# Retention attention and SoLU layer on one core: another written-out order of all steps

## The chip, the core and the metric

The kernel runs on one core of one Trainium2 chip. Its engines work at once, each through its own instructions in their order: TensorE (PE) multiplies matrices, VectorE (DVE) and ScalarE (ACT) work on what PE leaves in PSUM, GpSimd (POOL) works on SBUF alone, and SyncE (SP) starts nearly all DMA transfers. The metric is the device time of one execution in microseconds; lower is better. Three runs of the kernel before took 214.81, 215.29 and 213.99 us (median 214.81).

## What is computed

Inputs are q, k and v (8 batches, 8 heads, 576 positions, 64 values per head), two matrices of 512x1024 and 1024x512, and a scale vector. Attention without softmax, with a decay by distance, makes 4608 rows of 512; a layer of two products with a gated softmax and a normalisation between them makes the output, in float32.

```python
scores = scale * np.matmul(q, k.transpose(0, 1, 3, 2))
Dmat = np.where(rel >= 0, gamma[:, None, None] ** rel[None, :, :], 0.0)
attn = np.matmul(scores * Dmat[None, :, :, :], v)
x = attn.transpose(0, 2, 1, 3).reshape(B * S, H * D)
h = x @ w_in
sm = softmax(h)            # over the 1024 columns
solu = h * sm
ln = (solu - mean(solu)) / np.sqrt(var(solu) + 1e-06) * g_ln
out = ln @ w_out
```

## The kernel before

The 576 positions of a batch are cut into two pieces of 256 and a tail of 64. With 8 batches this gives 18 items: 0 to 3 are the first pieces of four batches, 4 to 7 their second pieces, 8 their four tails together; 9 to 17 are the same for the other four batches. Each item has two halves of 128 rows. The products are in float16 with sums in float32.

An item goes through named steps (the functions marked `@step`); a step's numbers are the item, the half, and sometimes a part:

- Loads on SP: `lq`, `lk`, `lv` fetch q, k and v of an item in float32 (512 KB each); `wi` and `wo` fetch quarters of the two matrices. All go through one ring of 16 buffers of 512 KB.
- Casts to float16: `q`, `k`, `v` on DVE, ACT or POOL, each half by itself (line 197 with a decay table, lines 150 and 152 plain); `cwA`, `cwB` cast the first matrix, `ws` and `cw` scale and centre the second (`mean`, `mc` make its column mean).
- Attention: `tp` transposes q and k on PE (32 small products, line 239) and `qkT` copies the result out of PSUM; for eight items `dt`, a transposing DMA on SP, does both. `kp` multiplies k by v into the running state (32 products, line 290), `t` and `s32` add and decay that state (lines 305 and 314), `s16` casts it. `sc` makes scores (16 products, line 265), `mk` applies the triangular mask on DVE (four per item, line 276), `xv` and `xs` multiply masked scores by v (32 products, line 364) and the state by q (4, or 8 for a tail, line 349). `xT` copies the result out as float16.
- Layer: `mm1` multiplies by the first matrix (8 products of 512 columns, line 426) into two PSUM banks; `max` takes the row maximum on DVE (line 434), `exp` the exponential and its sum on ACT (line 449), `solu` the gated product and its sum on DVE (line 497), `nmu` and `sq` mean and squares, `w1`, `w2`, `pow` the factor of each row. `lpj` (32 products, line 584) with the copies `uTj`, or two transposing DMAs `du`, transpose the result; items 0 to 2 are centred first by `uc`. `mm2` multiplies by the second matrix (8 products, line 607), `osb` scales by the factor (lines 619 and 623), `st` stores.
- `warm:k` puts k products of zeros (line 726) into the next PSUM bank, into which the next step writes anyway. Nothing reads them.

Nothing is scheduled by a compiler. One text, `ORDER`, lists some 1000 steps; a loop at the end of the kernel calls them in that order, and each engine gets its instructions in that order. A letter behind a step chooses the engine (`@v` DVE, `@s` ACT, `@g` POOL). So the text fixes, for each engine and for SP's queue alike, what stands behind what; semaphores then hold an instruction until its inputs are there and its buffer is free. A second text, `BANKS`, gives one digit for each PSUM bank that a step takes, in the order of the steps. PSUM has eight banks; `tp`, `sc`, `kp`, `lpj` and `mm1` take two each, the others one.

```python
for word in ORDER.split():
    word, _, eng = word.partition("@")
    name, _, n = word.partition(":")
    idx = [int(x) for x in n.split(".")] if n else []
    STEP[name](*(idx + [None] * 3)[:3], eng)
```

Of the kernel before, what the change touches and what calls it, by code (L numbers as in the profile page):

```python
# [46 lines left out]
def kernel(  # L47
# [684 lines left out]
    def gx_(n, i, j, eng):  # L732
# [23 lines left out]
        wo:3 k:3.0@s wo:2 max:1.1 wo:1 w2:0 uc:0.0@v xv:2 max:1.0 lk:5 xT:2.0@s xs:2.1 exp:1.1
        xT:2.1@v warm:2 mm1:2.0 lv:4 q:3.1@g ws:0@g lk:4 exp:1.0 ws:1@g pow:0 q:3.0@g solu:1.1
        max:2.0 ws:2@g lpj:0 solu:1.0 ws:7@s ws:4@s ws:6@s ws:3@s exp:2.0 warm:4 mm1:2.1 uTj:0.0@v
        uTj:0.1@v w1:1@g kp:3 t:3.0@s nmu:1.1 max:2.1 tp:3 ws:5@s qkT:3.1@s s32:3.0 qkT:3.0@s
        q:4.0@g k:5.0@g mean s16:3.0@g t:3.1 nmu:1.0 solu:2.0 uc:1.1@s sc:3.0 mc@s sc:3.1 k:4.0@g  # L760
        uc:1.0@v k:4.1@s exp:2.1 mm2:0.0 v:4.1@v mk:3.1.0 mk:3.0.0 mk:3.0.1 cw:6@v lv:5 sq:1.1
        cw:0@v tp:4 lq:5 mm2:0.1 xs:3.1 mk:3.1.1 v:4.0@g osb:0.0@s osb:0.1@v xv:3 qkT:4.1@s
        qkT:4.0@s lk:7 solu:2.1 lv:6 warm:4 kp:4 cw:5@g v:5.1@g w1:2@g v:5.0@g xT:3.0@v t:4.0
        sc:4.0 mk:4.0.1 warm:2 sc:4.1 q:5.1@g mk:4.1.0 lpj:1 nmu:2.0 mk:4.0.0 sq:1.0 lq:6 lk:6
        xT:3.1@s st:0.1 mk:4.1.1 s16:1.1@s mm1:3.0 s32:4.0 uTj:1.0@s nmu:2.1 w2:1 uc:2.0@v cw:1@v
        max:3.0 s32:3.1 q:5.0@g v:6.0@g uTj:1.1@s warm:2 mm1:3.1 k:5.1@s cw:7@v sq:2.0 k:6.1@g
        q:6.1@s exp:3.0 v:6.1@g k:7.1@s t:4.1 pow:1 kp:5 mm2:1.1 k:6.0@g q:6.0@g max:3.1 osb:1.1@s
        s16:4.0@g s32:4.1 t:5.0 mm2:1.0 solu:3.0 tp:6 exp:3.1 solu:3.1 xs:4.1 xs:4.0 s32:5.0 lq:9
        st:0.0 osb:1.0@s xv:4 qkT:6.0@s xT:4.0@s xT:4.1@s uc:2.1@v kp:6 lpj:2 dt:5 qkT:6.1@v t:6.0
        uTj:2.0@s sc:5.1 mm1:4.0 nmu:3.1 t:5.1 mk:5.1.1 cw:2@g cw:4@g cw:3@v uTj:2.1@s sq:3.1  # L770
        sq:2.1 w1:3@v mk:5.1.0 sc:5.0 mm1:4.1 lk:9 s32:6.0 mk:5.0.0 max:4.0 exp:4.0 w2:2 lq:7
        q:9.0@g mm2:2.1 pow:2 s16:2.1@g mm2:2.0 mk:5.0.1 lv:8 s16:5.0@g st:1.1 max:4.1 osb:2.1@s
        exp:4.1 solu:4.0 nmu:3.0 sc:6.1 t:6.1 osb:2.0@s xv:5 q:7.0@g lv:7 lk:8 xs:5.0 xs:5.1 sc:6.0
        k:7.0@s s16:6.0@g xT:5.0@s solu:4.1 mk:6.1.1 q:7.1@g k:9.0@s s32:5.1 k:9.1@g lpj:3 mm1:5.0
        mk:6.1.0 mk:6.0.1 lpj:4 xT:5.1@s sq:3.0 mk:6.0.0 lq:8 xv:6 xs:6.0 k:8.1@g w2:3 dt:7
        uTj:3.1@s uTj:3.0@v v:7.0@v max:5.0 uTj:4.0@s xs:6.1 st:1.0 exp:5.0 mm2:3.1 q:9.1@g mm2:3.0
        xT:6.1 v:7.1@g uTj:4.1@v s32:6.1 pow:3 s16:4.1@s nmu:4.0 kp:7 nmu:4.1 solu:5.0 s16:3.1@s
        osb:3.1@s sq:4.0 warm:2 sc:7.1 xT:6.0 v:8.1@g q:8.1@g k:8.0@g sq:4.1 osb:3.0@s t:7.0
        mk:7.1.1 sc:7.0 s32:7.0 q:8.0@g w1:4@g mk:7.0.0 mm1:5.1 tp:8 mk:7.0.1 t:7.1 qkT:8.0@s
        max:5.1 mm1:6.0 exp:5.1 mk:7.1.0 qkT:8.1@s nmu:5.0 mm2:4.1 st:2.1 lk:10 lv:9 lq:10 w2:4  # L780
        max:6.0 st:2.0 pow:4 mm2:4.0 exp:6.0 s16:7.0@g q:10.0@s solu:5.1 v:9.1@g s32:7.1 solu:6.0
        sc:8.0 osb:4.1@s xv:7 q:10.1@g mk:8.0.0 v:8.0@g mk:8.0.1 sc:8.1 osb:4.0@s lpj:5 sq:5.0
        xs:7.1 uTj:5.1@s mk:8.1.0 xs:7.0 xT:7.0@v nmu:5.1 xT:7.1@v v:9.0@g sq:5.1 uTj:5.0@s mm1:6.1
        mm1:7.0 w1:5@g k:10.1@g max:6.1 s16:5.1@g s16:7.1@g mm2:5.1 mm2:5.0 exp:6.1 nmu:6.0
        mk:8.1.1 max:7.0 lv:10 lq:12 w2:5 st:3.0 dt:9 solu:6.1 st:3.1 nmu:6.1 exp:7.0 w1:6@g lpj:6
# [128 lines left out]
```

## Time and profile before

The profile is of one execution of 215.09 us; its span, from the first to the last instruction of the program, is 213.4 us.

| What | Before |
|---|---|
| Median of three runs | 214.81 us (213.99 to 215.29) |
| Profiled execution / its span | 215.09 us / 213.4 us |
| PE busy | 198.1 us (93%) |
| DVE busy | 186.6 us (87%) |
| ACT busy | 171.9 us (81%) |
| POOL busy | 141.6 us (66%) |
| Share of 16 DMA engines used by SP's queue | 91.2% |
| Products of zeros (line 726) | 62, 17.8 us busy |
| Mean granted PE clock | 0.99 |

"Busy" joins the times of an engine's instructions. PE's instructions overlap, so eight products of 512 columns that show 381 ns each follow one another every 216 ns or so. In the list of groups, a row names the line, the engine and the operation, what is written and read with the shapes, how often, the busy time, the mean of one, and then how long the engine had been idle just before and what ended that idle time. In the chain of waits a row is start, length and what ran then; "issue" is time in which the engine waited for nothing that the profile shows. In the timeline a row is start, length, engine, line and operation, and in brackets the idle time before it.

### The profile page before, as it was taken

The page shows a single profiled execution, that of the slowest core. Times are in us where ns is not written, and L with a number is a line of the kernel's source. Part 1 is how long each engine was busy: PE and PEld are TensorE (multiplying, and loading weights), DVE is VectorE, ACT ScalarE, POOL GpSimd, SP SyncE. Part 2 cuts the span into 40 slices and gives each one's busy share as a digit, 9 for nine tenths or more (in the row PEclk, how much of TensorE's full clock was granted, in tenths as well). Part 3 has the DMA queues.
Part 4 walks back from the last instruction along what each step waited for, and adds up shares of the span by engine and source line. Part 5 has one row for each costly group of instructions (what it writes and reads, how often), then busy time and mean ns, then how long its engine had stood idle before and what let it go on. Part 6 is the DMA issues. An engine that isn't in the chain of part 4 may idle for free.

```text
span 213.4 us, 7652 instructions
## 1 busy us (share of the span) xinstructions
PE 198.1 (93%) x3166; PEld 104.4 (49%) x3166; DVE 186.6 (87%) x334; ACT 171.9 (81%) x290; POOL 141.6 (66%) x222
## 2 busy tenths in 40 slices
PE   4999879899989989999969999999999999999990
PEld 1444454445446454564635455554555455454560
DVE  3586879999999998899979899999999999698960
ACT  3245789899979897898986988999999973779981
POOL 6496989589999999495789893748564861001130
PEclk9999969999999999999999999999999999999999
DMA  6999999999699799998999999799975977562654
GB/s 163 290 386 309 276 301 389 293 278 283 208 230 216 161 163 275 293 222 234 315 308 298 163 314 318 142 260 252 226 212 131 238 98 199 98 151 50 196 197 100
DMA packets 90530, 49.29 MB, mean 231 GB/s; under 512 B 29440, under 2 KB 84992, under 8 KB 90496
## 3 DMA queue, kind: packets, MB, share of 16 engines
q1 hardware_dynamic: 90128, 48.70, 91.2%
q8 instruction: 24, 0.39, 0.9%
q10 hardware_dynamic: 368, 0.11, 0.3%
q14 instruction: 10, 0.08, 0.2%
HBM read 32.55 MB, written 9.44 MB: 197 GB/s over the span
## 4 chain that ended last, share of the span: by engine, by line
PE 73%; DVE 9%; DMA 6%; SPq 4%; issue 3%; POOL 3%; ACT 1%; DVEq 0%
PE psum L607 28%; PE psum L426 24%; DMA ld<-in_q_dram 6%; PE psum L265 5%; PE psum L364 4%; PE psum L349 3%; SPq L173 3%; PE psum L584 3%; DVE nm L434 2%; DVE u L497 2%; PE psum L290 2%; SPq L647 1%; PE psum L239 1%; PE psum L726 1%; DVE uc L553 1%
## 5 line engine op out<-in xcount | busy, mean ns | idle before, releaser
L426 PE MATMUL psum<-w_in,xT 128*128 128x512 f16 x280 | 66.4, 381 | 0.4 <-DVE w_in L152 0.3
L607 PE MATMUL psum<-w_out,uTj 128*128 128x512 f16 (+1 forms) x248 | 55.6, 372 | 0.0
L449 ACT ACTIVATE e<-psum,nm 128x1024 f32<-128x1024 f32 x35 | 38.9, 1113 | 11.3 <-DVE nm L434 10.3
L434 DVE TENSOR_REDUCE nm<-psum 128x1 f32<-128x1024 f32 x35 | 42.6, 1216 | 2.1 <-PE psum L426 1.9
L607 PEld LDWEIGHTS <-uTj 128*128 128x128 f16 x296 | 27.9, 98 | 30.6 <-issue 1.0
L497 DVE SCALAR_TENSOR_TENSOR u<-psum,e 128x1024 f16<-128x1024 f32 x35 | 42.3, 1215 | 0.6
L517 ACT ACTIVATE sq<-u,nmu 128x1024 f16<-128x1024 f16 x35 | 40.3, 1151 | 0.7 <-DVE nmu L507 0.5
L426 PEld LDWEIGHTS <-xT 128*128 128x128 f16 x280 | 25.6, 98 | 29.7 <-issue 1.4
L540 POOL TENSOR_TENSOR rs<-w,mhalf 128x2 f32<-128x2 f32 x17 | 11.8, 694 | 35.0 <-DVE w L528 34.8
L197 POOL TENSOR_TENSOR qk<-ld,small 128x512 f16<-128x512 f32 x27 | 28.5, 1059 | 3.8 <-DMA ld<-in_q_dram 3.5
L197 POOL TENSOR_TENSOR v<-ld,small 128x512 f16<-128x512 f32 x28 | 30.4, 1090 | 0.3
L726 PE MATMUL psum<-s16s 128*128 128x512 f16 x62 | 17.8, 424 | 3.6 <-DVE s16s L854 3.1
L314 POOL TENSOR_TENSOR s32a<-t,small 128x256 f32<-128x256 f32 x16 | 9.8, 611 | 12.6 <-DVE t L305 7.1
L265 PE MATMUL psum<-qkT 64*64 64x128 f16 x576 | 15.0, 225 | 2.1 <-issue 1.7
L150 ACT COPY uTj<-psum 128x1024 f16<-128x1024 f16 (+1 forms) x17 | 16.3, 982 | 0.7 <-PE psum L584 0.4
L152 POOL CAST qk<-ld 128x512 f16<-128x512 f32 x24 | 15.1, 642 | 0.4 <-DMA ld<-in_k_dram 0.3
L265 PEld LDWEIGHTS <-qkT 64*64 64x64 f16 x576 | 9.9, 109 | 9.6 <-issue 7.8
L150 ACT CAST xT<-psum 128x512 f16<-128x512 f32 x23 | 12.9, 591 | 1.6 <-PE psum L364 1.5
L150 ACT CAST qk<-ld 128x512 f16<-128x512 f32 x20 | 12.1, 614 | 2.5 <-DMA ld<-in_k_dram 2.5
L150 ACT COPY qkT<-psum 128x1024 f16<-128x1024 f16 x12 | 11.9, 1018 | 1.0 <-PE psum L239 1.0
L314 POOL TENSOR_TENSOR s32b<-t,small 128x256 f32<-128x256 f32 x16 | 9.8, 612 | 2.9 <-DVE t L305 1.9
L607 PE MATMUL psum<-w_raw,uTj 128*128 128x512 f16 x48 | 11.2, 380 | 0.5 <-DVE t L305 0.5
(262 smaller groups left out, 334.6 us busy)
## 6 DMA issues: line engine op xcount, KB each, us to landing
ld<-in_v_dram SPq DMA_DIRECT2D x16, 512.0 KB, 7.2
ld<-in_q_dram SPq DMA_DIRECT2D x16, 512.0 KB, 7.3
ld<-in_k_dram SPq DMA_DIRECT2D x16, 512.0 KB, 7.1
ld<-in_moe_w_in_dram SPq DMA_DIRECT2D x4, 512.0 KB, 7.7
ld<-in_moe_w_out_dram SPq DMA_DIRECT2D x4, 512.0 KB, 6.9
ld<-in_v_dram SPq DMA_DIRECT2D x8, 128.0 KB, 4.7
ld<-in_k_dram SPq DMA_DIRECT2D x8, 128.0 KB, 5.3
ld<-in_q_dram SPq DMA_DIRECT2D x8, 128.0 KB, 5.4
```

The lines of the kernel that those rows point to most:

```text
L150: nc.scalar.copy(out=out, in_=in_)
L152: vec(eng).tensor_copy(out=out, in_=in_)
L197: vec(eng).tensor_tensor(out=to, in0=src, in1=tab[:, 8 * e : 8 * e + 8].unsqueeze(2).to_broadcast([P, H, D]), op=ALU.mult,)
L265: nc.tensor.matmul(out=s[o][cc, hp], lhsT=qkT_view(n, 1, c)[dd, e, hp], rhs=qkT_view(n, 0, c)[dd, :, hp], start=True, stop=True,)
L314: nc.gpsimd.tensor_tensor(out=s, in0=T["t", n, i], in1=gs.unsqueeze(2).to_broadcast([P, 4, D]), op=ALU.mult)
L426: nc.tensor.matmul(out=h[:, a], lhsT=s[:, d], rhs=w_in16[:, d, a * 512 : (a + 1) * 512], start=r == 1, stop=r == 4,)
L434: nc.vector.tensor_reduce(out=nm, in_=T[key("h", n, i, j)], axis=AX.X if j is not None else AX.XY, op=ALU.max, negate=True)
L449: nc.scalar.activation(out=flat(e, j), in_=T[key("h", n, i, j)], func=ACT.Exp, bias=T["nm", n, i], accum_out=s)
L497: nc.vector.scalar_tensor_tensor(out=flat(u, j), in0=T[key("h", n, i, j)], scalar=1.0, in1=flat(T[key("e", n, i, j)], j), op0=ALU.mult, op ...
L517: nc.scalar.activation(out=t, in_=T[key("u", n, i, j)], func=ACT.Square, bias=T["nmu", n, i], accum_out=ss)
L607: nc.tensor.matmul(out=o, lhsT=T["uT", n, i][:, c], rhs=wt[:, c, a : a + w], start=c == 0, stop=c == NF - 1,)
L726: nc.tensor.matmul(out=junk, lhsT=zeros[:, 0:P], rhs=zeros, start=True, stop=True)
```

## The change

Only the two texts change. `ORDER` has the same steps but for the products of zeros: these were 62 in 13 places and are 50 in 8 places; 19 stood ahead of the first `tp`, now 21 do, and behind it 43 become 29. All other steps stand in another order. 68 steps change engine: among them `s16` (7 from POOL to ACT, 8 back), `k` (5 POOL to ACT, 6 ACT to POOL, 2 to DVE), `q` (3 POOL to DVE), `xT` (4 DVE to ACT, 3 back), `t` (2 DVE to ACT). The loads have another order too: the first is `lk:0` where it was `lv:0`. `BANKS` has other digits, of the same number. The beginning, some stretches further on, and the digits:

```diff
     ORDER = """
-        lv:0 lq:0 v:0.0@v q:0.0@g gx lk:0 lq:1 k:0.0@s q:0.1@v v:0.1@v k:0.1@g warm:19 tp:0 q:1.1@g
-        warm:4 kp:0 qkT:0.0@v qkT:0.1@v lk:1 wi:2 warm:2 sc:0.0 t:0.0@v q:1.0@g mk:0.0.0 wi:3
-        warm:3 sc:0.1 mk:0.0.1 k:1.0@g wi:1 mk:0.1.0 mk:0.1.1 k:1.1@g wi:0 s32:0.0 t:0.1 s16:0.0@g
-        warm:2 tp:1 cwB:2@s cwB:3@g s32:0.1 lv:1 xv:0 qkT:1.1@s qkT:1.0@v xT:0.0@s xs:0.1 cwA:3@s
-        sc:1.0 warm:8 sc:1.1 xT:0.1@s cwB:1@v cwA:2@s lq:2 cwA:1@v cwB:0@g cwA:0@v mk:1.1.1
-        mm1:0.0.2 g32 v:1.1@g mm1:0.1 mk:1.1.0 v:1.0@v mk:1.0.0 max:0.1 lk:2 mk:1.0.1 mm1:0.0.0
-        kp:1 q:2.0@g t:1.0@s mm1:0.0.1 mm1:0.0.3 s32:1.0 max:0.0 q:2.1@g k:2.0@g lv:2 s16:0.1@s
-        exp:0.1 t:1.1 v:2.1@v s16:1.0@g v:2.0@g k:2.1@s solu:0.1 warm:8 tp:2 lk:3 kp:2 t:2.0@v xv:1
-        xs:1.1 exp:0.0 lv:3 qkT:2.0@s lq:3 lq:4 qkT:2.1@s xT:1.0@s solu:0.0 nmu:0.1 s32:1.1 s32:2.0
-        xT:1.1@s sc:2.1 wo:0 v:3.0@g v:3.1@g sc:2.0 mm1:1.1 mk:2.1.1 t:2.1 nmu:0.0 mk:2.0.0
...
+        lk:0 gx lq:0 k:0.0@s k:0.1@g q:0.0@v lv:0 lq:1 q:0.1@v warm:21 tp:0 v:0.1@v v:0.0@v kp:0
+        q:1.1@v t:0.0@v s32:0.0 qkT:0.1@v qkT:0.0@s lk:1 k:1.0@v q:1.0@g warm:6 sc:0.0 t:0.1 wi:2
+        k:1.1@s sc:0.1 wi:0 wi:3 s32:0.1 mk:0.1.0 warm:4 tp:1 mk:0.0.0 mk:0.0.1 cwB:2@s s16:0.0@s
+        mk:0.1.1 xv:0 cwA:2@g wi:1 qkT:1.1@v cwA:0@v cwB:0@g xT:0.0@v cwB:3@g qkT:1.0@s sc:1.0
+        mk:1.0.1 xs:0.1 cwA:3@s mm1:0.0.3 lv:1 cwA:1@g xT:0.1@v s16:0.1@g cwB:1@s v:1.1@g mk:1.0.0
+        sc:1.1 mm1:0.0.0 lq:2 lk:2 q:2.1@g q:2.0@g mk:1.1.0 mm1:0.1 v:1.0@v mk:1.1.1 k:2.0@g
+        max:0.1 exp:0.1 mm1:0.0.2 mm1:0.0.1 max:0.0 k:2.1@v kp:1 t:1.0@s warm:7 tp:2 s32:1.0 lv:2
+        solu:0.1 v:2.1@v exp:0.0 s16:1.0@g qkT:2.1@s qkT:2.0@s t:1.1 v:2.0@g nmu:0.1 solu:0.0
+        xs:1.1 lq:4 xv:1 lv:3 lq:3 lk:3 xT:1.0@s nmu:0.0 warm:2 sc:2.1 sc:2.0 mk:2.1.0 xT:1.1@s
+        kp:2 q:4.1@g q:4.0@g s32:1.1 mk:2.0.0 t:2.0@s mk:2.1.1 mk:2.0.1 uc:0.1@s sq:0.1 mm1:1.1
...
+        sc:4.1 q:6.0@s q:6.1@s mk:4.0.1 v:5.1@g mm2:1.0 exp:3.0 max:3.1 st:0.1 lv:6 mk:4.1.0
+        mk:4.1.1 mm2:1.1 xv:4 w1:2@g xs:4.1 v:6.0@g solu:3.0 k:6.0@s v:6.1@g osb:1.0@s exp:3.1
+        solu:3.1 dt:5 kp:5 t:5.0 osb:1.1@s xs:4.0 tp:6 st:1.0 s16:2.1@g cw:1@v st:0.0 sq:2.0 kp:6
+        xT:4.1@s t:6.0 warm:2 lpj:2 s32:5.0 qkT:6.1@v t:5.1 xT:4.0@s qkT:6.0@s uTj:2.1@s cw:4@g
+        sc:5.1 sc:5.0 uTj:2.0@s nmu:3.1 lq:8 mk:5.1.1 cw:7@v mk:5.1.0 sq:3.1 k:7.0@s sq:2.1 cw:3@v
+        mk:5.0.0 mm1:4.0 max:4.0 lv:8 cw:2@g w2:2 pow:2 s32:6.0 mm1:4.1 s16:5.0@g exp:4.0 s16:6.0@g
...
     BANKS = "".join(
         """
-        765473652176543201675354327654730167542354017654764532765426573102634127605704352713045760
-        173765432105672431732654301542376541073624501765432714053675342015427651034765201765437653
-        201765423475410326501457637210345763201763275463107567342017436520175642346571045762310745
-        760162376546501764532765476
+        765432765174630175237654736452316754230154673245345210765421076540156732473214065327640126
+        743025143761275463764521067531235076432016523767510643254016574237654103256743201765365721
+        034756201675436721045673210547623765401675473256107347652017654320176542365410756320174356
+        742340165746523765437653276
         """.split()
     )
```

More of the change, by code (lines that the diff above doesn't have):

```diff
@@ L756 @@
[L756 to L785, printed above, removed]
@@ L816 @@
-        w2:11 solu:12.1 t:15.1 xv:14 nmu:12.1 kp:16 solu:13.0 xs:14.0 sq:12.1 t:16.0 w2:12 mm1:13.1
-        pow:11 osb:11.1@s s32:15.1 s16:12.1@g s32:16.0 s16:11.1@g sc:15.1 xT:14.0 xT:14.1 nmu:13.0
-        sc:15.0 du:12.1 s16:16.0@g s16:15.0@s osb:11.0@s t:16.1 max:13.1 mk:15.0.1 pow:12 mk:15.0.0
-        s16:13.1@s mk:15.1.1 mm1:14.0 mm2:12.0 s16:15.1@s dt:16 exp:13.1 xs:15.1 st:11.1 mm2:12.1
-        max:14.0 mk:15.1.0 solu:13.1 s32:16.1 xv:15 st:11.0 sc:16.1 osb:12.0@s sq:13.0 osb:12.1@v
@@ new lines @@
+        w1:10@g sq:10.0 q:16.0@g q:14.0@s mk:13.1.1 mk:13.1.0 lk:17 st:8.0 xT:12.1 osb:9.1@s
+        osb:9.0@s mm1:11.1 max:11.1 sq:10.1 lpj:10 nmu:11.0 sc:13.0 mk:13.0.0 mk:13.0.1 w2:10
+        uTj:10.1@s uTj:10.0@s exp:11.1 lv:16 lv:15 mm1:12.0 max:12.0 exp:12.0 s16:13.0@g xs:13.1
+        tp:14 v:15.1@g s32:13.1 mm2:10.1 qkT:14.0@v xv:13 solu:11.1 xs:13.0 pow:10 qkT:14.1@s kp:14
+        xT:13.1@s sc:14.0 xT:13.0@s solu:12.0 nmu:11.1 mk:14.0.1 osb:10.1@s sc:14.1 w1:11@v t:14.0
+        sq:11.0 mm2:10.0 mm1:12.1 lk:16 mk:14.1.1 v:15.0@g st:8.1 lv:17 osb:10.0@s k:16.0@g
```

118 lines of the change are left out of this document (70 added, 48 removed).

## Prediction, made before the changed kernel was seen

> **What bounds the kernel now.** I read the page's shares first, then busy time by stage, then the start in the timeline, then the chain of waits. The page:
>
> ```profile
> span 213.4 us, 7652 instructions
> ...
> PE 198.1 (93%) x3166; PEld 104.4 (49%) x3166; DVE 186.6 (87%) x334; ACT 171.9 (81%) x290; POOL 141.6 (66%) x222
> ...
> DVE  3586879999999998899979899999999999698960
> ...
> PEclk9999969999999999999999999999999999999999
> ...
> q8 instruction: 24, 0.39, 0.9%
> ```
>
> PE is busy in nearly every slice, DVE from the sixth on; the granted clock falls once, in the slice from 26.7 us. PE's code comes as 24 packets of 16 KB; its 6332 recorded instructions make that 256 each, that is 128 products with their weight loads. A chain that says "PE" does not yet say that PE is the cause, so I cut the span into stages (columns: stage, length, then busy time and instructions of PE, weight loads, DVE, ACT, POOL; clock, DMA share, GB/s):
>
> ```profile
> 0.00:31.80 31.80, 26.04 (x425) 13.14 (x426) 21.82 (x36) 16.61 (x26) 23.99 (x44) 0.95 1.04 287
> 31.80:85.00 53.20, 50.22 (x889) 26.55 (x891) 52.53 (x89) 48.16 (x80) 49.13 (x64) 1.00 1.00 250
> 85.00:205.00 120.00, 118.25 (x1855) 62.58 (x1843) 110.97 (x207) 104.32 (x181) 67.39 (x113) 1.00 0.90 215
> ```
>
> Three stages with three limits. Until 31.8 us all 16 DMA engines are taken (share 1.04) while PE has 5.8 us idle and DVE 10.0: data arrival sets the pace. From 31.8 to 85 us DVE is busy 52.53 of 53.20 us: DVE sets it, and the products of zeros fill some of what PE has left over. From 85 to 205 us PE is busy 118.25 of 120.00 and DVE 110.97: PE sets it.
>
> **The start, where the orders differ most.** Rows of the timeline (start, length, what, in brackets idle time and what ended it):
>
> ```profile
> 3.11 6.53 PE L726 MATMUL psum<-s16s 128*128 128x512 f16 x19 [3.11 <-DVE s16s L854]
> ...
> 5.12 0.69 DVE L197 TENSOR_TENSOR v<-ld,small 128x512 f16<-128x512 f32 x1 [1.92 <-DMA ld<-in_v_dram]
> ...
> 6.93 0.69 DVE L197 TENSOR_TENSOR qk<-ld,small 128x512 f16<-128x512 f32 x1 [1.11 <-DMA ld<-in_q_dram]
> ...
> 8.75 0.62 ACT L150 CAST qk<-ld 128x512 f16<-128x512 f32 x1 [2.49 <-DMA ld<-in_k_dram]
> ...
> 9.56 0.64 PE L239 MATMUL psum<-ident,qk 64*128 64x64 f16 x32
> ...
> 10.58 2.05 POOL L197 TENSOR_TENSOR qk<-ld,small 128x512 f16<-128x512 f32 x2 [1.04 <-DMA ld<-in_q_dram]
> ...
> 17.66 1.93 DVE L152 CAST w_in<-ld 128x512 f16<-128x512 f32 x3 [1.70 <-DMA ld<-in_moe_w_in_dram]
> ...
> 21.98 1.22 DVE L434 TENSOR_REDUCE nm<-psum 128x1 f32<-128x1024 f32 x1
> ...
> 22.52 1.05 POOL L197 TENSOR_TENSOR qk<-ld,small 128x512 f16<-128x512 f32 x1 [0.16 <-DMA ld<-in_q_dram]
> ...
> 25.98 0.69 DVE L197 TENSOR_TENSOR v<-ld,small 128x512 f16<-128x512 f32 x1 [0.69 <-DMA ld<-in_v_dram]
> ...
> 26.59 1.22 DVE L497 SCALAR_TENSOR_TENSOR u<-psum,e 128x1024 f16<-128x1024 f32 x1
> ...
> 28.11 0.62 PE L290 MATMUL psum<-v,qk 64*64 64x64 f16 x32 [1.94 <-POOL v L197]
> ...
> 28.75 0.42 DVE L152 COPY t<-psum 128x256 f32<-128x256 f32 x1 [0.94 <-PE psum L290]
> ```
>
> Transfers land one behind the other: first at 5.1 us, second 6.9, third 8.7, fourth 10.5, eighth 17.6, eleventh 22.5, thirteenth 25.9, so one load of q, k or v takes about 1.75 us. The new order keeps the kinds in these places (five loads, four quarters of the first matrix, eight loads, four quarters of the second, loads again) and only changes which tensor takes which, so landing times stay. Followed step by step, with these durations:
>
> First `tp`: k:0 and q:0 are now loads 1 and 2, so the casts are done at about 8.3 us (6.93 plus two of 0.69) instead of 9.5. But 21 products of zeros stand ahead instead of 19, and 19 last until 9.64. Start about 9.9 us against 9.56: no gain, a loss of 0.3.
>
> First `max`: the last quarter of the first matrix is transfer 9 in both, one quarter behind the row at 17.66, about 19.0 us. Its last cast is now on POOL behind another one; the products follow. 22.0 to 22.7 us against 21.98; I take 22.2. The 8 products of zeros dropped between `sc:1.0` and `sc:1.1` bring nothing here, since `mm1` waits for the matrix. `tp:2` needs load 11 (22.5), two casts of q at 1.05 and one of k on POOL: 25.2 us, as before.
>
> Then a gain. Before, DVE waited 0.94 us for `t:2.0`, behind `kp:2`, which waited 1.94 us for a cast of v on POOL; `solu:0.0` stood behind it on DVE.
>
> ```profile
> 29.09 1.22 DVE L497 SCALAR_TENSOR_TENSOR u<-psum,e 128x1024 f16<-128x1024 f32 x1
> ...
> 31.75 0.14 DVE L507 TENSOR_SCALAR nmu<-su 128x1 f32<-128x1 f32 x1
> 31.81 0.68 DVE L276 TENSOR_TENSOR ret__702<-psum,tris 128x512 f16<-128x512 f32 x1
> 32.41 0.68 DVE L276 TENSOR_TENSOR ret__704<-psum,tris 128x512 f16<-128x512 f32 x1
> ```
>
> In the new order `t:2.0` is on ACT, `kp:2` comes behind `sc:2`, and nothing on DVE waits for it. From 22.2 us: two `max` of 1.13 (21.98 to the next DVE step at 23.11), a cast of k 0.6, `solu:0.1` 1.14 (29.09 to 30.23), the cast of load 13 (25.95, not late), `t` 0.33, `solu:0.0` from 27.2 to 28.4, `nmu:0.0` at 28.5 against 31.75. ACT does `t:2.0` in 0.4 us between two copies; if it is late there, `uc:0.1` is queued behind it. DVE has then done 0.7 us more of its work than before at `nmu:0.0` (the casts q:0.0, q:1.1, k:1.0, k:2.1 are added, two `qkT` copies and two casts of the matrix gone), so it is 3.25 + 0.7 = 3.9 us ahead.
>
> **The DVE stage.** I end it where `mm2:3.1` begins, since the same useful products stand ahead of it in both orders. DVE's steps ahead of that point differ in few: gone are `cwA:1`, `cwB:1`, `uTj:3.0`, `t:2.0`, `xT:2.1`, `v:7.0` and two `qkT`, 4.5 us at the pitch of like rows (0.60 for a copy or mask, 31.81 to 32.41); added are two k, three q, `v:7.1`, one `qkT`, three `xT`, one `w1`, 6.1 us. So 1.6 us more lies in DVE's way: 3.9 - 1.6 = 2.3 us earlier at best. Lower end: at `mm1:4.1`, some 11 us of products earlier, the new order has 3.4 us more DVE work ahead, which leaves 0.5. I take 1.5, between the two, the better end being the one beside `mm2:3.1`. The other engines hide behind this: POOL has 49.13 of 53.20 us busy in this stage and its total rises by some 3 us over the kernel (added up with like rows), mostly as two casts of the matrix at the start, where it waited for loads; ACT has 48.16 and its total falls by 1 us. If POOL loses that cover, `kp` and `tp` are late next.
>
> **The PE stage.** Behind `mm2:3.1` no useful product is added or removed. Chain of waits:
>
> ```profile
> 79.45 1.00 issue
> ...
> 81.39 3.45 PE psum L607 x16
> ...
> 103.07 0.57 PE psum L584 x32
> 103.64 0.38 PE psum L290 x32
> 104.02 0.57 PE psum L239 x32
> 104.59 0.57 PE psum L364 x32
> ...
> 108.22 1.71 issue
> ...
> 115.51 0.22 PE psum L349 x4
> ...
> 187.06 1.73 PE psum L426 x8
> ...
> 189.02 0.35 PE psum L265 x16
> ```
>
> Before, two things in this stage are not useful work: the 1.71 us pause at 108.22, which the profile can't explain by a wait, and one pair of zero products ahead of `sc:7.1`, 2 x 0.22 = 0.4 us (a product of 512 columns is 1.73/8). The pause and the one at 79.45 us stand exactly 512 products apart, four code packets: PE waited for its next packet. I count along both orders in steps of 128 products, with the chain's prices (`mm1`, `mm2` 1.73, `tp`, `xv`, `lpj` 0.57, `kp` 0.38, `sc` 0.35, `xs` 0.22). The 160 products ahead of the two pauses are 4.9 and 5.1 us of work; the next shortest stretches, 6.05 and 6.1 us, show no such pause. In the new order the stretch ending near `sc:9.0` is 6.2 us, so the 1.71 goes. Two short ones remain: 4.7 us ending in `xv:6` and 4.95 us ending in `lpj:2`; both lie in the DVE stage, where 1.0 us each has cover, and where the first answers to the pause at 79.45. I count them at nothing beyond the 1.5 us taken instead of 2.3.
>
> The Trainium skill ("Runtime: NRT & Kernel Launch", section "Instruction fetch mechanics") says that code comes in blocks of 256 instructions and that fetching is mostly hidden. The trace agrees on the size and not on the hiding, with 1.00 and 1.71 us.
>
> **Zero products.** They are 12 fewer:
>
> ```profile
> L726 PE MATMUL psum<-s16s 128*128 128x512 f16 x62 | 17.8, 424 | 3.6 <-DVE s16s L854 3.1
> ```
>
> 43 behind the first `tp` become 29; 14 x 0.216 = 3.0 us, but a filler's time is gained only where what it covered is gone. Of these 3.0 us, 0.4 is counted above and the rest lies in the first two stages, where data and DVE decide: counted at nothing, with 0 and 2.6 as ends. The tail keeps its steps and nearly their order; DVE and ACT have idle time there, so I take 0, with 0.5 on either side.
>
> **Sum.** 1.5 (DVE stage) + 1.7 (packet) + 0.4 (zeros) - 0.3 for new waits on banks and buffers that the trace can't show (bounded by the 0.4 and 0.5 us waits that it does show on PE) = 3.3 us. Span 213.4 - 3.3 = 210.1; execution 215.09 - 3.3 = 211.8. That execution stands 0.28 above the median, so I give 211.6 us, 1.5% less.
>
> **The rivals.** *Nothing gained:* arrival of data sets the start, and landing times stay; the removed zero products turn into waits, and the DVE stage starts where it did. For it: `tp:2` at 25.2 in my own working. Against: the 0.94 and 1.94 us waits of DVE and PE are not on data of that moment's DMA. Then only the packet's 1.7 moves, and the extra 1.6 us on DVE takes it back: 214.8.
>
> *Slower, by late code.* The new order packs small steps: one packet (`xv:4` to `lpj:2`) is 2.6 us of work, one from `sc:3.1` 3.8. At the pause at 79.45 a packet's 128 products took 5.67 us from end to end:
>
> ```profile
> 74.78 0.22 PE L364 MATMUL psum<-ret__1595,v 64*64 64x128 f16 x2
> ```
>
> ```profile
> 80.45 0.21 PE L364 MATMUL psum<-ret__1771,v 64*64 64x128 f16 x1 [1.00 <-issue]
> ```
>
> If a packet can't take less than that, these lose 5.7 - 2.6 = 3.1 and 5.7 - 3.8 = 1.9 us, and if DVE waits for PE there, it is 211.6 + 5.0 = 216.6. It decides from about 4.2 us of such loss. Against: long products stand ahead of both, and before, a packet with `mm2:10.0` in it was through in 5.5 us of work without a pause.
>
> *The pauses are not code.* They are known as "issue" alone, and two at a distance of four packets may be chance. Then the 1.71 us stays: 211.6 + 1.7 = 213.3. For it: other boundaries pass with no pause. Against: no wait of any engine ends there. The skill's section named above would be right on the hiding.
>
> *Slower clock.* After the wait at 26.2 us the clock fell:
>
> ```profile
> 26.00:29.00 3.00, 1.06 (x64) 1.04 (x60) 2.06 (x4) 2.55 (x4) 2.48 (x4) 0.86 1.15 291
> 29.00:32.00 3.00, 3.00 (x63) 1.93 (x56) 2.57 (x8) 2.40 (x4) 2.75 (x5) 0.57 1.15 309
> ```
>
> 0.43 of 3 us is 1.3 us lost. With fewer zero products PE may have another such gap in the DVE stage, at 1.3 us plus what DVE then waits: about 213.1. For it: 2.6 us less filling. Against: DVE, not PE, sets that stage. The Trainium skill ("TensorE: Matmul & The Clock Gate", "Part 1: The HAM clock gate") says that an idle window of about 3.4 us halves the clock; the trace agrees, with 1.06 us busy of 3.00 ahead of the fall, and it speaks against leaving out fillers.
>
> **Chances.** Forecast 0.46, pauses not code 0.06, slower clock 0.10, nothing 0.14, late code 0.24. Faster by over 0.5% is the first three, 0.62. The forecast's own range is 209.3 to 213.6: below, 0.8 for the DVE stage at 2.3, half of the 2.6 us of zeros and the 0.3 of new waits; above, 1.0 for the DVE stage at 0.5, 0.5 for the first `max` at 22.7 and 0.5 in the tail. The runs before span 1.3 us, 0.6%, so 0.5% is about what can be told. The range reaches from 209.3 into the late code, to 216.2.
>
> **What would show it.** `nmu:0.0` near 28.5 us and a DVE without gaps from there; `mm2:3.1` near 79.9; no pause of "issue" between 100 and 115 us; at most 1.7 us of pauses near 57 and 80; PE dense from 85 us. Wrong if DVE is not ahead at `nmu:0.0`, if PE has several pauses of over 1.5 us with a packet's end behind them, or if the clock row shows a second low slice.

## The result, and the profile after

The changed kernel takes 213.44 us in the median of 16 runs (211.04 to 215.40), the kernel before 214.13 us in 16 runs beside them. The ratio is 0.9932 with a 95% interval of 0.9903 to 0.9961: 0.7% faster, about 1.5 us. It leaves out the slow executions, those over 1.5% above the fastest of their kernel (4 of the 16 after); the medians of all 16 are 0.7 us apart. In a later set with 12 runs the ratio was 0.9957 (0.9913 to 1.0002). The forecast was 211.6 us, 3.2 us less than the median of three runs that it started from; by the ratio, something under half of that came. The 16 runs of the kernel before have a median 0.7 us under those three. The profiled execution after took 214.05 us with a span of 212.3 us; before it was 215.09 and 213.4.

The head of the page after (engines' shares, then 40 slices of 5.3 us):

```profile
span 212.3 us, 7613 instructions
...
PE 196.4 (93%) x3154; PEld 103.2 (49%) x3154; DVE 186.1 (88%) x335; ACT 171.0 (81%) x288; POOL 143.6 (68%) x223
...
DVE  3499699999998999898979999999998999798960
...
PEclk9996799999999999999999999999999999999999
...
q8 instruction: 24, 0.39, 0.8%
```

The shares say nearly nothing: PE 196.4 instead of 198.1 us. The clock row says more: it is low in the slices from 16 to 26 us, where the kernel before had full clock, and full in the slice from 26.7, where that one fell. Busy time by stage after (columns as before: length, busy time of PE, weight loads, DVE, ACT, POOL, clock, DMA share, GB/s):

```profile
0.00:31.80 31.80, 25.21 (x416) 12.17 (x417) 23.06 (x37) 15.62 (x23) 19.53 (x39) 0.89 1.04 287
31.80:85.00 53.20, 49.18 (x857) 26.49 (x857) 52.30 (x87) 48.22 (x77) 50.95 (x64) 1.00 0.93 236
85.00:205.00 120.00, 119.26 (x1863) 62.69 (x1862) 109.61 (x210) 105.48 (x185) 72.52 (x121) 1.00 0.94 221
```

The three limits stand as before. Two readings stand out. First the chain of waits in the start (start, length, what ran):

```profile
18.61 1.01 PE psum L426 x2
19.62 0.57 PE psum L265 x12
20.19 4.37 PE psum L426 x10
24.56 0.02 issue
24.58 1.24 DVE nm L434
...
29.34 0.40 PE psum L349 x4
```

Ten products of `mm1` take 4.37 us, 0.44 us each, twice the 0.22 us that they take elsewhere: PE runs at half clock, and the first `max` comes at 24.58 instead of 21.98 us. Second, the pauses of "issue" later in the same chain:

```profile
66.00 0.90 issue
...
80.73 0.73 issue
82.09 3.45 PE psum L607 x16
...
109.90 0.74 issue
111.68 3.45 PE psum L607 x16
```

The 1.71 us behind `sc:9.0` became 0.74 us, the pause in `xv:6` is still there with 0.73 us for 1.00, and one of 0.90 us in `lpj:2` is new.

### The profile page after: what moved, and what is told of

Read it like the earlier page. It is cut to its first block, busy times and chain, and to the rows that moved or that the text cites. A ratio compares the mean times of both kernels' runs of the same rounds, so it can differ in the third digit from the quotient of the medians.

```text
span 212.3 us, 7613 instructions
## 1 busy us (share of the span) xinstructions
PE 196.4 (93%) x3154; PEld 103.2 (49%) x3154; DVE 186.1 (88%) x335; ACT 171.0 (81%) x288; POOL 143.6 (68%) x223
## 4 chain that ended last, share of the span: by engine, by line
PE 70%; DVE 14%; DMA 4%; SPq 4%; issue 3%; ACT 2%; POOL 1%; ACTq 0%; DVEq 0%; POOLq 0%
PE psum L426 25%; PE psum L607 24%; PE psum L265 5%; DVE nm L434 4%; PE psum L364 4%; DMA ld<-in_moe_w_in_dram 4%; PE psum L349 3%; PE psum L584 3%; SPq L173 3%; DVE u L497 2%; PE psum L290 2%; PE psum L239 1%; SPq L647 1%; PE psum L726 1%; DVE uc L553 1%
## 5 line engine op out<-in xcount | busy, mean ns | idle before, releaser
L426 PE MATMUL psum<-w_in,xT 128*128 128x512 f16 x280 | 68.5, 390 | 1.6 <-issue 0.7
L197 POOL TENSOR_TENSOR qk<-ld,small 128x512 f16<-128x512 f32 x24 | 25.0, 1050 | 1.1 <-DMA ld<-in_q_dram 0.6
L150 ACT COPY uTj<-psum 128x1024 f16<-128x1024 f16 (+1 forms) x18 | 17.3, 990 | 3.1 <-PE psum L584 3.1
L314 POOL TENSOR_TENSOR s32a<-t,small 128x256 f32<-128x256 f32 x16 | 10.6, 662 | 11.8 <-DVE t L152 6.9
L726 PE MATMUL psum<-s16s 128*128 128x512 f16 x50 | 14.2, 429 | 3.5 <-DVE s16s L853 3.1
L364 PEld LDWEIGHTS <-v 64*64 64x64 f16 x576 | 9.3, 106 | 7.1 <-issue 6.8
L349 PE MATMUL psum<-qkT,s16s 128*128 128x128 f16 (+1 forms) x128 | 10.7, 216 | 1.6 <-POOL s16s L152 1.4
```

The costliest lines, as they stand in the source:

```text
L150: nc.scalar.copy(out=out, in_=in_)
L197: vec(eng).tensor_tensor(out=to, in0=src, in1=tab[:, 8 * e : 8 * e + 8].unsqueeze(2).to_broadcast([P, H, D]), op=ALU.mult,)
L314: nc.gpsimd.tensor_tensor(out=s, in0=T["t", n, i], in1=gs.unsqueeze(2).to_broadcast([P, 4, D]), op=ALU.mult)
L349: nc.tensor.matmul(out=to, lhsT=state[:, hp].rearrange("p e d -> p (e d)"), rhs=rhs, start=first and hp == 0 and j == 0, stop=True, skip_g ...
L364: nc.tensor.matmul(out=x[c][oo, hp], lhsT=v16[cc, e, 2 * hp + o], rhs=T["ret", n, e, o][cc, hp], start=first[c] and e == 0 and hp == 0, st ...
L426: nc.tensor.matmul(out=h[:, a], lhsT=s[:, d], rhs=w_in16[:, d, a * 512 : (a + 1) * 512], start=r == 1, stop=r == 4,)
```

## Where the two kernels stand, step by step

Each experiment below changed the kernel before or the changed kernel in one or two places. This table takes one profiled execution of each: start of the first `max`, of `nmu:0.0`, of `mm2:3.1` (where the DVE stage ends) and of the last item's `mm2`, all in us; then PE's idle time before a matmul that the waits put down to "issue", in us; and the ratio to the kernel before, run in the same set, with its 95% interval.

| Kernel | first max | nmu:0.0 | mm2:3.1 | last mm2 | PE "issue" | Ratio |
|---|---|---|---|---|---|---|
| before | 21.98 | 31.75 | 81.22 | 207.53 | 2.7 | |
| changed | 24.58 | 30.59 | 81.93 | 206.75 | 2.4 | 0.9932 (0.9903-0.9961) |
| changed, again (e5) | 23.40 | 29.40 | 80.61 | 204.63 | 1.1 | 0.9957 (0.9913-1.0002) |
| e1 before, no 8 zeros | 23.19 | 32.20 | 82.17 | 210.88 | 4.2 | 0.9994 (0.9952-1.0036) |
| e2 changed, filled | 22.06 | 28.23 | 80.29 | 207.20 | 3.5 | 0.9981 (0.9946-1.0016) |
| e3 changed, shifted | 23.69 | 29.69 | 80.14 | 207.01 | 1.8 | 1.0011 (0.9978-1.0044) |
| e4 filled and shifted | 22.01 | 28.29 | 78.74 | 205.00 | 1.5 | 0.9963 (0.9928-0.9999) |
| e6 filled, packets clear | 21.75 | 28.26 | 78.41 | 203.15 | 0 | 0.9924 (0.9891-0.9957) |
| e7 before, packets clear | 22.97 | 32.00 | 80.47 | 205.05 | 0.2 | 0.9930 (0.9895-0.9965) |
| e9 as e6, not filled | 23.38 | 29.38 | 79.82 | 205.12 | 0.2 | 0.9916 (0.9876-0.9955) |
| e10 as e6, kp:2 moved back | 21.95 | 30.43 | 86.90 | 211.56 | 0 | 1.0261 (1.0182-1.0339) |
| e11 as e6, fewer cuts | 21.98 | 28.40 | 78.84 | 203.56 | 0 | 0.9888 (0.9838-0.9937) |
| e12 as e7, 8 more zeros | 21.82 | 33.95 | 82.30 | 208.19 | 0 | 1.0021 (0.9985-1.0057) |

Single executions of one kernel differ by 2 to 4 us, so a row shows where time goes, and the ratio shows what it is worth. The row of e1 is the longest of its twelve executions, 218.44 us with a mean granted clock of 0.971; its other eleven took 212.68 to 216.09 us.

## Experiments: the clock in the start, and the packets

The theory after the first look had two causes. *Clock:* the dropped zero products left PE idle between 14.6 and 18.6 us, the granted clock fell, and `mm1` of item 0 ran at half speed. *Late packets:* PE's code arrives in packets of 256 instructions, and PE waits where the 128 products ahead of a packet take too little time. The rivals: data sets the start and the zeros don't matter, and the pauses belong to the steps in which they stand.

**e1: the 8 zero products taken out of the kernel before.**

```diff
-        sc:1.0 warm:8 sc:1.1
+        sc:1.0 sc:1.1
-        warm:19 tp:0
+        warm:11 warm:16.256 tp:0
```

(`warm:k.256` is k products of zeros of 256 columns; two of them take the time of one full one.)

> Kernel before, with the 8 zero products between sc:1.0 and sc:1.1 taken out, and the first 19 zero products replaced by 11 full ones and 16 of half width (the same TensorE time there, and the same number of products in all, so that the instruction packets keep their places). Theory 'clock': TensorE then idles for about 1.7 us ahead of mm1 of block 0, the granted clock falls in the windows 16 to 28 us (before: 1.00, 0.99 and 0.57 only at 28 to 32), the products of mm1:0.1 take up to 0.43 us each instead of 0.22, max:0.1 comes near 24.5 instead of 21.98, and the kernel is 0.5 to 2 us slower than before. Theory 'arrival' (what the prediction said): mm1 waits for the matrix anyway, the clock stays, max:0.1 stays at 21.9 to 22.2, the time stays within 0.3 us.

Measured: first `max` at 23.19, and the granted clock fell right behind PE's idle time, in windows of 4 us:

```profile
16.00:20.00 4.00, 1.68 (x36) 0.83 (x25) 2.23 (x4) 2.74 (x4) 2.12 (x3) 0.96 1.11 317
20.00:24.00 4.00, 4.00 (x43) 1.54 (x42) 2.83 (x5) 0.00 (x0) 3.33 (x4) 0.61 1.08 279
```

The same windows had 3.55 and 3.96 us of PE and a clock of 1.00 in the kernel before. So without the zeros the clock fell here, in one long execution; over e1's twelve the mean clock goes from 0.971 to 1.000, so the fall doesn't come every time. (0.7 us of PE's idle time is a late packet, up to 17.02 us; 1.4 us, up to 18.79, is the wait for the matrix.) The ratio, 0.9994 (0.9952 to 1.0036), shows no loss in time that is clear of noise. Of the 1.2 us lost at `max`, 0.45 us is left at `nmu:0.0`: DVE no longer waits 0.69 us for a load at 25.98 us, nor 0.43 us for an `xT` at 30.81, both waits of the kernel before. The wait of `kp:2` for POOL's v takes up nothing; it is as long as before (1.89 us for 1.94) and ends 1.0 us later. The prediction's sentence on these zeros fails on the clock, and no run shows it wrong for the time of *this* order.

**e2, e3, e4: the changed kernel filled, shifted, both.** e2 puts 9 zero products back:

```diff
-        mk:0.1.1 xv:0
+        mk:0.1.1 warm:7 xv:0
-        cwA:3@s mm1:0.0.3
+        cwA:3@s warm:2 mm1:0.0.3
```

e3 leaves PE's time alone and cuts zero products in two, so that each later product stands 38 products further on in the code (e4 does both, with the same 38 in all):

```diff
-        warm:21 ... warm:6 ... warm:4 ... warm:7
+        warm:42.256 ... warm:12.256 ... warm:8.256 ... warm:14.256
```

> Changed kernel with zero products back in the idle time of TensorE in the start: 7 ahead of xv:0 and 2 ahead of mm1:0.0.3 (9 x 0.213 us = 1.9 us). Theory 'clock': the granted clock stays near 1.0 from 16 to 26 us, max:0.1 at 22.2 to 22.8 instead of 24.58, nmu:0.0 near 28.5 instead of 30.59, and the time is 0.8 to 2 us under the changed kernel's, with less spread between its runs. Theory 'arrival': nothing changes at the start, within 0.3 us of the changed kernel (213.4, 0.7% under the kernel before). The 9 products also move the packet boundaries 9 products earlier, by which the theory 'late packets' expects the pause at lpj:2 (0.90 us) to shrink to 0.5 us or less and the one at xv:6 (0.73 us) to stay or grow a little.

> Changed kernel with the first 38 zero products cut in two (76 of half width): the same TensorE time, but every later product stands 38 instructions pairs later, so that the boundaries of the 256-instruction packets fall on other products. Theory 'late packets': the pauses at lpj:2 (66.90, 0.90 us) and at xv:6 (81.46, 0.73 us) go, since the 128 products ahead of the new boundaries hold more work there; one pause of 0.7 to 1 us near sc:9.0 stays or moves to within 38 products of it; 0.5 to 1.6 us faster than the changed kernel. Rival 'waits of those steps': the pauses belong to lpj:2, xv:6 and sc:9.0 themselves (their operands or banks), stay at the same steps with the same 0.7 to 0.9 us, and the time stays within 0.3 us.

> Changed kernel with both: the 9 zero products in the idle time of the start, and half-width zeros in the start so that the boundaries stand where e3_shift has them (38 products). Theories 'clock' and 'late packets' together: the gains add, 1.3 to 3 us under the changed kernel, near 211 (1.5 to 2% under the kernel before). If only the clock counts, the same as e2_fill; if only the packets count, the same as e3_shift; if neither, as the changed kernel, 213.4.

The clock theory holds in the trace. Changed kernel, then e2:

```profile
12.00:16.00 4.00, 2.84 (x75) 1.67 (x77) 3.88 (x7) 2.79 (x5) 3.31 (x5) 1.00 1.03 408
16.00:20.00 4.00, 3.15 (x69) 1.69 (x68) 4.00 (x7) 2.91 (x3) 3.24 (x4) 0.70 1.11 316
20.00:24.00 4.00, 4.00 (x18) 1.40 (x11) 2.75 (x4) 0.00 (x0) 3.28 (x5) 0.50 1.15 284
```

```profile
12.00:16.00 4.00, 4.00 (x78) 2.06 (x77) 3.70 (x8) 3.31 (x6) 3.87 (x5) 1.00 1.02 406
16.00:20.00 4.00, 3.45 (x78) 1.78 (x76) 3.98 (x8) 2.54 (x3) 2.72 (x3) 1.00 1.12 315
20.00:24.00 4.00, 4.00 (x50) 1.83 (x49) 3.74 (x5) 0.79 (x2) 3.70 (x6) 1.00 1.09 275
24.00:28.00 4.00, 2.21 (x60) 1.26 (x61) 4.00 (x8) 3.76 (x7) 3.81 (x6) 1.00 1.01 270
```

In the window from 20 us PE runs 50 matmuls instead of 18. `nmu:0.0` is at 28.23 and 28.29 us in e2 and e4, 2.3 us earlier than in the first profile of the changed kernel and 1.1 us earlier than in its second (e5).

The packets follow the code, not the steps. Rows of the timeline with the idle time in brackets, in the order e2, e3, e4:

```profile
64.59 0.39 PE L584 MATMUL psum<-ident,uc 64*128 64x64 f16 x15 [0.63 <-issue]
...
79.70 0.21 PE L364 MATMUL psum<-ret__1812,v 64*64 64x128 f16 x1 [1.02 <-issue]
...
108.87 0.22 PE L290 MATMUL psum<-v,qk 64*64 64x64 f16 x4 [1.86 <-issue]
```

```profile
108.92 0.24 PE L265 MATMUL psum<-qkT 64*64 64x128 f16 x1 [1.83 <-issue]
```

```profile
107.17 0.24 PE L265 MATMUL psum<-qkT 64*64 64x128 f16 x1 [1.49 <-issue]
```

With the code shifted by 38 products (e3, e4) the pauses in `lpj:2` and `xv:6` are gone, as forecast; with 9 (e2) they stay (0.63 us in `lpj:2`, where 0.5 or less was expected), and the place behind `sc:9.0`, with little work ahead of it at all these shifts, pauses for 1.5 to 1.9 us. The expectation for e3, 0.5 to 1.6 us faster than the changed kernel, fails by that: 1.1 us at 108 us went against the 1.6 us gained at 66 and 81. e2 loses the same 1.1 us there and another 0.8 us at 158 us, where in that execution POOL's casts have fallen behind two loads of 8.8 and 9.7 us. All three ratios lie between 0.996 and 1.001, none under the changed kernel's 0.9932, so the gains expected for e2 (0.8 to 2 us) and e4 (1.3 to 3 us) failed as well, and what the causes are worth was not yet to be read from the times.

One thing can be read: e4 reaches `mm2:3.1` 1.55 us ahead of e2, with `nmu:0.0` at the same time in both. That is nearly the sum of the two pauses that e2 has in the DVE stage, 0.63 and 1.02. At `tp:8`, 4 us on, 1.1 us of it is left (84.44 against 83.33): a third of the pauses had cover, not the whole.

## Experiments: packets clear of every short stretch

e6 is the changed kernel filled (with 6 more zero products ahead of `xs:1.1`), zero products in the start halved, and the products of 11 steps between 85 and 120 us cut in two, which moves the packets there once more. The arithmetic is the same:

```diff
+    CUT1 = {(5, 1), (6, 0), (6, 1), (7, 0), (8, 1)}
+    CUT2 = {(4, 0), (4, 1), (5, 0), (5, 1), (6, 0), (6, 1)}
-        for c in range(NF):
-            nc.tensor.matmul(out=o, ... rhs=wt[:, c, a : a + w], ...)
+        for z in (slice(0, 256), slice(256, 512)) if (n, i) in CUT2 else (slice(0, w),):
+            for c in range(NF):
+                nc.tensor.matmul(out=o[:, z], ... rhs=wt[:, c, a : a + w][:, z], ...)
```

and `mm1` likewise for CUT1. e7 does the same to the kernel before and leaves its order as it is: zeros halved (44 products more) and 8 steps cut between 79 and 100 us. e5 is the changed kernel itself.

> The changed kernel once more, beside the others of this set. Theory 'late packets': the pauses stand at the same three places (packets that begin in lpj:2, xv:6 and behind sc:9.0), but the one behind sc:9.0, 0.73 us in the first profile, is nearer the 1.5 to 1.9 us that e2_fill and e3_shift had there with the same 4.1 to 4.4 us of work ahead of it; theory 'clock': the granted clock is under 0.8 in one or two of the windows between 16 and 28 us, max:0.1 between 23.5 and 24.6. Time 213 to 213.7, 0.3 to 0.9% under the kernel before.

> Changed kernel with the idle time of the start filled (7 and 2 zero products, and 6 more ahead of xs:1.1), half-width zero products in the start, and the products of 11 steps between 85 and 120 us each cut into two of half the width, so that the boundaries of the packets miss every short stretch. Theory 'late packets': no pause of over 0.5 us at lpj:2, xv:6 or sc:9.0, mm2:3.1 near 78.7 as in e4_fill_shift, and sc:9.0 to the end 1.5 us shorter than there: span near 209.4, time near 211, 1 to 2% under the kernel before. If the halved products cost TensorE time of their own, up to 0.05 us for each of the 11 steps, 0.5 us less is gained. If the pause behind sc:9.0 is not code, it stays at 1.5 to 1.9 us and the time is that of e4_fill_shift, 213.4 to 213.8.

> Kernel before with its order untouched, and only the boundaries of its packets moved: half-width zero products in the start (44 products more in the same time) and 8 steps between 79 and 100 us cut into products of half the width. Theory 'late packets': the pauses of 1.00 us at xv:6 and 1.71 us behind sc:9.0 go; the second lies on TensorE's own path and is gained whole; of the first, what the prediction said (cover in the DVE stage) gives nothing, while e3_shift and e4_fill_shift against e2_fill speak for the whole 1.0. So 1.7 us by the prediction and 2.7 us if pauses of the DVE stage count too: 0.8 or 1.3% under the kernel before. Rival 'not code': the pauses stay at their steps and the time is within 0.3 us.

e7 is the clean test, since only the place of the packets, and the cuts that move it, differ from the kernel before. Its ratio is 0.9930 (0.9895 to 0.9965): 1.5 us, as much as the whole change gave. The waits of the kernel before list these two for "issue" ahead of matmuls (line waited for: us in total, times, longest us):

```profile
PE psum L265 <- issue: 1.7, 1, 1.7
PE psum L364 <- issue: 1.0, 1, 1.0
```

and those of e7:

```profile
PE psum L265 <- issue: 0.2, 1, 0.2
```

`sc:9.0` and `mm1:8.0` now run on:

```profile
107.33 0.40 PE L265 MATMUL psum<-qkT 64*64 64x128 f16 x16
107.66 1.90 PE L435 MATMUL psum<-w_in,xT 128*128 128x512 f16 x8
109.39 0.81 PE L617 MATMUL psum<-w_out,uTj 128*128 128x512 f16 x3
```

In the trace both pauses come back whole: `nmu:0.0` is 0.25 us later than before, `mm2:3.1` 0.75 us earlier, so 1.0 us between them, and from there to the last `mm2` it takes 124.58 instead of 126.31 us, 1.73 less. The larger of the two expected gains (2.7 us, if pauses of the DVE stage count too) fits the trace; the timed gain of 1.5 us, 0.7 to 2.2 by its interval, leaves both it and 1.7 possible.

e6 has no pause at all, 0.9924 (0.9891 to 0.9957), 211.92 us in the median; 211 was expected. Its profiled execution, with a span of 208.7 us, is the shortest of its twelve, whose mean is 210.25. At `mm2:3.1` it leads e5 by 2.20 us; at `tp:8` by 1.76 (83.00 against 84.76), since PE, ahead of the others, waits between the two; at the last `mm2` by 1.48. So in these two executions the 11 cut steps cost about 0.3 us at most.

e5 shows how much the pauses vary from one execution to the next: 0.50, 0.58 and none where the first profile had 0.90, 0.73 and 0.74. The expectation of 1.5 to 1.9 us behind `sc:9.0` was wrong for it, and its clock fell less, to 0.81 and 0.77 in the windows from 16 and 20 us.

## Experiments: what the filling, the moved kp:2 and the order are worth

> As e6_packets, but without the 15 zero products in the idle time of the start; the boundaries of the packets are held in place by narrower zero products ahead of tp:0, sc:0.0, tp:1 and tp:2 (of 256 and 128 columns, the same TensorE time there). Theory 'clock': the granted clock falls to 0.5 to 0.7 in one or two windows between 16 and 28 us, max:0.1 comes at 23.4 to 24.6 instead of 21.8, nmu:0.0 at 29.4 to 30.6 instead of 28.3, and the time is 1 to 2 us over e6_packets. Rival: the start's loss is caught up by the 85 us at which TensorE becomes the limit, and the time is within 0.4 us of e6_packets.

e9 drops the 15 zeros of e6 and keeps the packets in place:

```diff
-        warm:42.256 ... warm:14.256 xv:0 ... warm:2 mm1:0.0.3 ... warm:6 xs:1.1
+        warm:27.256 warm:30.128 ... xv:0 ... mm1:0.0.3 ... xs:1.1
```

The clock fell to 0.83 and 0.74 at 16 to 24 us, and `nmu:0.0` came at 29.38 instead of 28.26. In the same set e11, which is filled, has 28.40 and 78.84 against 29.38 and 79.82: 0.98 us lost at `nmu:0.0`, 0.98 us lost at `mm2:3.1`. Nothing is caught up in the DVE stage. The ratios, 0.9916 (0.9876 to 0.9955) against 0.9888 (0.9838 to 0.9937), are 0.6 us apart, with intervals that overlap. So the rival's mechanism falls in these two traces, and the size in time stays open: the intervals allow e11 to be some 2 us faster or 0.8 us slower.

The mean granted clock of every execution is on record and says more. In the 18 of e6 and e11, which are filled, it is never under 0.994; in the 12 of e9 it goes from 0.981 to 0.999, in the 28 of the changed kernel from 0.973 to 1.000. So the clock doesn't fall in every execution of the changed kernel, and the first profile, at 0.983, is the second lowest of its 16. The time goes with it: of the first 16, the three at 1.000 took 211.22 to 212.54 us, and the three lowest that the ratio counts, at 0.983 to 0.986, took 213.51 to 214.05. This is a correlation, and a mean doesn't say where in the span the clock fell.

> As e6_packets, but with kp:2 back ahead of the two sc:2 (behind v:2.0) and t:2.0 on VectorE right behind it, as in the kernel before, and the banks of kp:2, sc:2.1 and mm1:1.1 chosen anew so that none waits for the end of block 0. The prediction's step: VectorE loses 0.7 us (t:2.0) and more behind the wait for kp:2, nmu:0.0 comes 1.2 to 2.6 us later than in e6_packets (28.3), mm2:3.1 at 79.9 instead of 78.4, and the end 1.5 us later. Rival: the same work follows in any case and what t:2.0 costs VectorE there it saves later; mm2:3.1 and the end move by less than 0.4 us.

```diff
-        v:2.0@g nmu:0.1 ... warm:2 sc:2.1 sc:2.0 ... kp:2 ... mk:2.0.0 t:2.0@s
+        v:2.0@g kp:2 t:2.0@v nmu:0.1 ... warm:2 sc:2.1 sc:2.0 ... mk:2.0.0
```

With `kp:2` back in its old place PE stands 2.55 us for POOL's cast of v, the wait of the kernel before, and `nmu:0.0` comes 2.17 us later than in e6:

```profile
28.22 0.45 PE L290 MATMUL psum<-v,qk 64*64 64x64 f16 x32 [2.55 <-POOL v L197]
```

That is the prediction's step, in the upper half of the 1.2 to 2.6 us expected for it. What follows can't be used: the banks that I chose anew make `xv:2` wait for a `max` and `t:2.1` for an `exp`, PE stands another 5 us by 43 us, and the end is 8.4 us late. A first form (e8) kept the banks as they were; there `kp:2` overwrote a bank of item 0 ahead of its last reader, so it computes something else, and its time isn't used. How much of the 2.17 us reaches the end was therefore not measured by itself.

> As e6_packets, with 7 steps cut into halves instead of 11 (and 10 zero products behind 40 us halved in their place). e6_packets took 124.7 us from mm2:3.1 to mm2:17.1.0 against 124.0 in e5_changed, neither with a pause behind sc:9.0, so a cut step costs about 0.06 us: 0.2 to 0.3 us faster than e6_packets if no pause comes back. The stretch near 139 us has 5.2 us of work for its packet again: theory 'late packets' allows 0 to 0.5 us there, so between 0.3 faster and 0.3 slower than e6_packets, 1 to 1.5% under the kernel before.

e11 cuts 7 steps instead of 11. No pause came back, and it takes 124.72 us from `mm2:3.1` to the last `mm2`, as e6 (124.74): the expected 0.2 to 0.3 us did not show. At 0.9888 (0.9838 to 0.9937), 211.86 us in the median of 6 runs, it is level with e6 and the best version here: ahead of the kernel before, and 0.9 and 1.6 us under the changed kernel's two medians (212.74 and 213.44, from other sets), with intervals that overlap.

> e7_before_packets (order of before, boundaries of the packets moved) with 8 more zero products ahead of xv:1, where TensorE waits 1.9 us at 26 to 29 us and the granted clock falls to 0.57 behind it. Theory 'clock': the clock stays near 1.0 at 28 to 32 us, and 0.3 to 1 us is gained over e7_before_packets (1.8 us under the kernel before), since only the part of the loss that VectorE did not cover counts. What is then left between this and e6_packets is what the new order itself is worth, with clock and packets out of the way: by the prediction's steps 1.5 us in the DVE stage plus 0.4 us of zero products; rival, from the mean spans of e6_packets and e7_before_packets (210.25 and 210.54): 0 to 0.3 us.

```diff
-        warm:16.256 tp:2 lk:3 kp:2 t:2.0@v xv:1
+        warm:8 tp:2 lk:3 kp:2 t:2.0@v warm:8 xv:1
```

A miss, and mine: PE's wait in this order stands ahead of `kp:2`, and I put the zeros behind it. They ran after the wait, at a lowered clock, in the way of `xv:1` (chain of waits):

```profile
27.80 0.45 PE psum L290 x32
28.25 2.80 PE psum L737 x8
31.04 1.00 PE psum L364 x16
```

`nmu:0.0` is 1.95 us later than in e7, `mm2:3.1` 1.83 us, and the ratio goes from 0.9930 to 1.0021, the whole gain of the packets. Outside the idle stretch this filler cost its full time, and nearly all of the delay at 30 us was still there at the end of the DVE stage.

What the new order is worth with the packets out of the way is e6 against e7: 2.1 us at `mm2:3.1` and 1.9 us at the last `mm2` in the profiled executions, and 0.9924 against 0.9930 in the times of one set, which is no difference that can be told. Why the times show so little of it is not settled; the spans of e6's executions spread over 3.4 us with the clock at 0.994 or more in all, so something beside the clock and these pauses varies. The two loads that came late in e2 are a candidate that no run here tested.

## Why the prediction was right or wrong

The direction was right and the range held the time; the gain was less than half of the forecast's. The time, 213.44 us, is nearest to two rivals that had small chances: "the pauses are not code" at 213.3, which the runs rule out, and "slower clock" at 213.1, whose mechanism the traces do show. Two of the prediction's own signs went against it in the first profile: a pause of "issue" between 100 and 115 us, and a second low slice in the clock row. In the second profile both are absent.

**Start.** The first `tp` lost a little, as said. The first `max` was put at 22.2 us (22.0 to 22.7); it came at 24.58 and, in the second profile, 23.40. The step that failed is "The 8 products of zeros dropped between `sc:1.0` and `sc:1.1` bring nothing here, since `mm1` waits for the matrix". In the profiles they brought the clock. With nine products put back `max` was at 22.0 and 22.1, where the forecast had it. The rival of the slower clock was named, but placed in the DVE stage at 1.3 us; it struck some 10 us earlier and cost 1.1 to 2.3 us at `nmu:0.0`. The Trainium skill ("TensorE: Matmul & The Clock Gate", "Part 1: The HAM clock gate") puts the fall after an idle window of about 3.4 us; here PE was busy 2.84 of 4 and 3.15 of 4 us around it, in short waits, and the clock fell all the same.

**DVE 3.9 us ahead.** `nmu:0.0` was put at 28.5 us. The changed kernel has 30.59 and 29.40; with the clock held it is 28.23 to 28.40 in e2, e4, e6 and e11. The mechanism (`kp:2` behind `sc:2`, `t:2.0` on ACT) was right, and e10 brought the old wait back; the size came only where the clock was held.

**DVE stage.** 1.5 us was taken of 2.3. Without pauses and with the clock held the order reaches `mm2:3.1` at 78.4 to 78.8 us, and the old order without pauses at 80.47: 1.6 to 2.1 us, as forecast. What failed is the cover, "both lie in the DVE stage, where 1.0 us each has cover": the short stretches ending in `lpj:2` and `xv:6` were seen, sized at 4.95 and 4.7 us of work, and counted "at nothing beyond the 1.5 us taken instead of 2.3". These sizes count 160 products, but a packet is 128, and over 128 the same prices give 2.6 us (the prediction's own figure for its late-code rival) and 4.1. They paused 0.90 and 0.73 us (0.50 and 0.58 in the second profile), nearly all of it visible at `mm2:3.1` and two thirds at `tp:8` (e4 against e2). The 0.8 us held back from the stage's 2.3 made the pauses good. That it fits is luck, since 1.5 was taken as a value between 2.3 and 0.5 and not from the length of the pauses. From `nmu:0.0` to `mm2:3.1` the forecast had 51.4 us, the changed kernel took 51.3 with its pauses, and e4, e6 and e11 took 50.2 to 50.5 without.

**The pause behind `sc:9.0`.** "So the 1.71 goes" was nearly right: 0.74 us is left in one profile and nothing in the other. Here too the 6.2 us of work counts more than a packet; over its 128 products the chain's prices give 5.4. From `mm2:3.1` to the last `mm2` the changed kernel takes 124.82 and 124.02 us instead of 126.31, a gain of 1.5 to 2.3 against the 2.1 of packet and zeros together. The rival "the pauses are not code" falls with e3, e4 and e7.

**The sum.** For the profiled execution: 2.2 us late at `mm2:3.1` (81.93 against 81.22 less 1.5), nearly all of it from the start; 0.6 us more from there to the last `mm2` (124.82 against 126.31 less 2.1), which is about the pause that was left; 0.3 us less in the tail, and 0.3 us that the forecast had put aside for new waits. That makes the 2.2 us between 210.1 and 212.3. (By its own terms the forecast's last step gives 211.5, not 211.6.) Of "slower, by late code", the place and the cause were right and the size was not: `xv:4` to `lpj:2` lost 0.5 to 0.9 us instead of 3.1, and the packet from `sc:3.1` lost nothing, its 128 products running through in 4.26 us in both profiles.

## What to carry to other kernels

Count the instructions of the busiest engine: where 128 products run in under 5 to 6 us, its next packet may not be there, though some stretches of 3.8 to 4.8 us passed here without a pause. Moving such a boundary (by cutting a filler or a long product in two) gained 0.7% with the order untouched, as much as a rewritten order of a thousand steps. Before a filler is dropped, ask what it does for the clock of the products behind it, and put one only where the trace shows idle time, since behind the wait it costs all of its length (2.80 us in e12). This kernel's second stage, in which DVE, ACT, POOL and PE are all over 90% busy, has little cover: delays of 1.0 and 1.9 us at its start arrived at its end whole or nearly, and pauses of 1.6 us inside it with two thirds.
